# The order of the first two batches: what runs when, and where idle products stand

## The chip, the core and the metric

The kernel runs on one core of a Trainium2 chip. The metric is the device time of one execution in microseconds (us). A core has five engines that run their own instruction queues in order and wait for each other by semaphores: PE (TensorE, matrix products), DVE (VectorE), ACT (ScalarE), POOL (GpSimd) and SP (SyncE, which here issues every load and store).

## The reference

Eight batches. In each, two attentions follow each other: 32 packed queries p attend to the 576 positions of k and v, and then the 576 queries q attend to the 32 packed results. Then a layer with three maxima, and an output layer.

```python
batch, n_heads, seq, head_dim = (8, 8, 576, 64)
n_pack = 32
...
def sm_attn(qq, kk, vv):
    s = scale * np.matmul(qq, kk.transpose(0, 1, 3, 2))
    s = s - np.max(s, axis=-1, keepdims=True)
    a = np.exp(s)
    a = a / (np.sum(a, axis=-1, keepdims=True) + 1e-09)
    return np.matmul(a, vv)
p_packed = sm_attn(p, k, v)
out = sm_attn(q, p_packed, p_packed)
...
h = np.maximum(np.maximum(x @ w1, x @ w2), x @ w3)
return (h @ w_out).astype(np.float32)
```

Here x is `out` with heads and batches laid out as 4608 rows of 512, w1 to w3 are 512 x 768, and w_out is 768 x 512.

## The kernel before

The whole program is a list of generators, and two strings of words say in which order they are advanced: START (lines 48 to 73) for batches 0 and 1 and the first steps of batch 2, LOOP (line 76) once for each batch from 2 on, with steps of the next batches among its own. `run` (line 619) takes a word, finds or begins its generator, and lets it issue instructions up to its next `yield`. There is no other scheduler: each engine's queue holds its instructions in the order of the words. A trailing v, g or a puts a step on DVE, POOL or ACT in place of its default.

The words, with batch b, row half r, column block j:

- k, v, q, w: loads by SP. `w02` is the third part of weight block 0, `w6x` is w_out. `q010` is one half of the positions of q.
- Sb, `scores` (line 243): products of p and k, 32 of them, into two PSUM buffers.
- Abr, `weigh_and_turn` (line 605), four steps: maximum over 576 and its negated factor (L266, L267, DVE), exponential with its sum (L271, ACT), transposes of the result (L296, L297, PE), copies (a1t, `copy`).
- Zbr: the inverse of the sum. Vbr, `values` (line 324): products with v, 40 for each r (L337), and pp. Kb, `packed`: one transpose (L352) and the copy to pt.
- Qb, `queries` (line 356): products with q. In batch 0 it has two steps, one for each half of the positions.
- Bbrh, `attend` (line 374): the second softmax, step by step: transposes from PSUM (L389), maxima (L393), subtraction (L395), exponential (L397), sums (L400), inverse, product (L409), transpose (L412), split into high and low part (a2h, a2l).
- Cjc, `convert` (line 177): each weight part is turned into its form by two ACT steps, a shift on DVE (L202) and an add on POOL (L206).
- Pbj, `project` (line 424): products of pt and a weight block (L439), and their split into ph (ACT) and pl (DVE).
- Nbj, `layer_in` (line 459): groups of six products (L475, 36 for each b and j). E: the running maxima. H: operands of the output layer. W: its weights. O, F: the output layer and its end.

Buffers matter here. Scores, second scores, and batch 1's transposes take turns on two large PSUM buffers (`ps_big`), so a step that writes one waits until the last reader of its former contents is done. k, v, q and a few intermediate tiles share eight buffers, staged weights six. SP keeps eight loads under way, and the ninth waits for the first.

A word In (`idle`, line 136) lets the next PE step that calls `rouse` (line 138) first issue n idle products of 128 columns, of the identity matrix with itself. They write the buffer that the step will fill next, in groups of at most 512 columns.

```python
def rouse(ps):
    k = ps.shape[-1] // P
    for i in range(0, idle[0], k):
        n = min(idle[0] - i, k)
        nc.tensor.matmul(
            out=ps[:, 0:n * P], lhsT=ident, rhs=ident.unsqueeze(1).to_broadcast([P, n, P]),
            start=True, stop=True,
        )
    idle[0] = 0
```

Of the kernel before, what the change touches and what calls it, by code (L numbers as in the profile page):

```python
# [45 lines left out]


START = """
k00 k01 w02 I10 S0 A00 A00 k10 w00 C00 k11 Z00 w22 A00 w01 A01 A01 v01 Z01 C00 C02 C00 C01 v00 I4 S1 A10 A10
q000 C00 A11 I7 A01 A01v V01 C02 C02 A00v Z10 C01 C01 V01 q010 V00 C02 V00 K0 A11 Z11 C01 C22 C22 C22 K0 I1 Q0  # L50
B000 C22 B000 B000 B000 B010 B010 B000 q011 q001 I8 Q0 B011 B010 B010 w12 B001 B000v B000 B000g C12 I3 P00 P00
k20 B001 k21 B011 v11 B001 w10 B011 B010 B010 B000 B000g P00 P00 B001 B011 C12 C12 S2 B001 B000 B001 v10 B001
w11 B010 A21 B001g q10 q11 A21 I10 N00 A20 A20 B011 B010g B010 C12 B011 B011 B011g A10 A11 A10 A11 w21 C11 C11
V101 B010v C10 C10 B011 P00 B001 B001v w20 V101 B010 N00 E000 K1 w32 C11 K1v C10 N00 Q1 B001v C11 B10 C21 B11
C21 E000 E000 C20 N00 C10 P01 P01 B011g C21 C20 w42 C20 C32 w52 P01 B011 P10 X2 N00 N00 E001 E001 C32 C32 C42
C42 C42 C52 C21 w31 N01 E010v C20 w30 C31 C31 E001 B11 N01 v20 E010 N01 P02 C32 E010 C42 C31 C31 N01 w41 N01
w40 P02 P02 C30 E011 E011 C52 C52 N01 C30 P10 C30 X2 C41 C41 N02 P10 E011 N02 E020 E020 C30 B10 N02 C40 C41
Z21 E020 P03 P03 N02 E021 N02 w50 C50 C52 P03 N02 N03 N03 B10 w51 E021 E021 H01 N03 C50 C50 C40 C40 H00v B10
C41 B10 B10 B10 B11v N03 E031v C51 C51 C40 P04 E030v C51 C51 P11 P04 w64 B11 X2 E030 N03 N03 P04 N04 E031 E040
B11 B11 H02v N04 H02 C50 P05 v21 B10g E040 B11 B10 E031 C64 P05 B11g N04 N04 B11 B11 w61 N04 E041v C64 B10g  # L60
P05 B10 N04 C64 B11 w65 C61 w63 V201 E041 C65 C65 E040 E041 H04 H04 N10 E100v C65 N10 C61 C61 E100 Z20 V201
E030 N10 N10 N10 N10 C65 E101v P11 P11 N11 C64 q20 E101 q21 E101 w60 C60 C61 C60 E100 H04v E110v C60 C60 N11
N11 E110 E110 H10 N11 E111 W2v K2 w62 N11 E111 H10g K2 W0v W0 Q2 B20 B21 N11 N05 C63 H01v H00 C62 C62 C62 P13
E050 C63 W0v E111 B20 P12 P12 N05 C62 N05 N05 W0 E050 W2v E050 P12 W0v W2 N05 N05 N12 E051 H00 C63 C63 P13 W1
E120 N12 N12 E051 E051 N12 N12 W0 P14 B21 W2 P13 E120 E120 H03 P15 W2v W2g N12 E121 E121 W0v H01 W1 W1 W1 H02
N13 E121 N13 E130v E130 N13 N13 P14 N13 W1v W1 O0 P14 F0 E130 B20 O0 E131v N13 E131 H03v N14 N14 W1v H03v E131
W1v P15 B21 N14 E140v E140 W1g W1 W2v B21 B21 E140 F0 N14 O0 E141v P15 F0 O0 N14 N14 H05 H05v B20 H05v E141
H03 F0 H01 N15 O0 H12 N15 B20 H05 H13 E150v H01 W0 W2 O0 E141 F0 k30 F0 H03 H01v H14 H05 N15 N15 E151 E150
H03v N15 H05v E150 N15 O0 O0 H12 W0g E151 E151 H15 H13 H12v F0 O0 W2 H14 H13v W0v k31 F0 F0 O0 O0 O0 F0 F0 W2
O0 F0 F0 F0 H10v H14v H11 O0 O1 F1 O1 O1 F1 F1 B20v H15v F0 H15 B21 H11v H11v H13v H13 F0 H13v P20 H11 H11 P20  # L70
P20 H15 P22 P21 B21 P20 P20 O1 F1 H11v H15v O1 O1 H15v F1 F1 O1 B20 B20g O1 O1 F1 O1 F1 F1 B21g B21 B21 O1 F1
F1 O1 P22 P22 B21 P21 O1 F1 B20 P21 F1 B20 O1 F1 F1 B20v F1
"""


# [612 lines left out]
```

## Time and profile before

| | |
|---|---|
| median of 3 runs | 472.93 us (472.85 to 473.01) |
| the profiled execution: its time | 472.98 us |
| its span in the profile | 471.2 us |
| PE busy, share of the span | 457.2 us, 97% |
| DVE, ACT, POOL busy | 343.6, 168.4, 218.6 us |
| mean granted TensorE clock | 0.991 |
| DMA, GB/s in the first 47 us, in slices of 11.8 us | 332, 373, 379, 285 |

The profiled execution is a single one, and its span is measured from the first to the last recorded instruction. PE's share is close to full, but idle products count as busy, and so do products at a lower clock. Times within the execution are counted from the start of the span. "mi" are the products of the layer, "mo" those of the output layer, "s" scores of either kind, "tp" transposes, "av" products with v, "pw" projections. The figure in brackets at a row's end is the engine's idle time ahead of it and what ended it. In a row, x32 counts instructions, and an f32 product is two of them. The granted clock is given as a share of full speed.

### The profile page before, as it was taken

To read this page: it belongs to the slowest core of one execution; us is meant where nothing else is said; L and a number is where in the kernel's file an instruction comes from. 1 tells how busy PE (TensorE), PEld (TensorE's weight loads), DVE (VectorE), ACT (ScalarE), POOL (GpSimd) and SP (SyncE) were. 2 spreads that over 40 slices of the span, in tenths; PEclk is the share of its full clock that TensorE was granted. 3 is DMA by queue.
4 is the path that set the end of the run, shared out by engine and by line. 5 is a ranking of instruction groups with operands and counts; after the bars stand their busy time and mean duration, and the time that the engine had idled before them with its cause. 6 is when DMAs were issued, how large, how long until landed. Compare 5 with 4: busy or idle time off the path is not lost.

```text
span 471.2 us, 11512 instructions
## 1 busy us (share of the span) xinstructions
PE 457.2 (97%) x4710; PEld 404.1 (86%) x4710; DVE 343.6 (73%) x722; ACT 168.4 (36%) x325; POOL 218.6 (46%) x193
## 2 busy tenths in 40 slices
PE   7799999999999999999999999999999999999996
PEld 2447887899989898989989898998989898998996
DVE  1669986987888678786777678776787667875652
ACT  3458855634233226122350225212260223402330
POOL 0467784776544055612564037421556036531642
PEclk9889999999999999999999999999999999999999
DMA  8998856002213640082303730064300820020002
GB/s 332 373 379 285 293 159 245 1 1 86 86 65 119 199 127 1 25 282 51 111 1 101 229 105 35 26 204 118 120 1 34 280 41 3 26 75 1 1 4 98
DMA packets 36580, 55.66 MB, mean 118 GB/s; under 512 B 17328, under 2 KB 27568, under 8 KB 36528
## 3 DMA queue, kind: packets, MB, share of 16 engines
q1 hardware_dynamic: 36528, 54.93, 35.4%
q8 instruction: 37, 0.61, 0.5%
q14 instruction: 15, 0.12, 0.1%
HBM read 41.94 MB, written 9.44 MB: 109 GB/s over the span
## 4 chain that ended last, share of the span: by engine, by line
PE 87%; DMA 6%; DVE 3%; ACT 1%; issue 1%; POOL 1%; SPq 1%; DVEq 0%; ACTq 0%; POOLq 0%
PE mi L475 45%; PE mo L544 29%; PE pw L439 7%; DMA wi<-in_wi 3%; DMA v<-in_va 2%; PE av L337 2%; DMA wi<-in_wo 2%; PE s L366 2%; PE s L253 1%; PE s L143 1%; DVE e L389 1%; DVE w_sb L202 1%; DVE r L489 0%; DVE xt L218 0%; PE tp L296 0%
## 5 line engine op out<-in xcount | busy, mean ns | idle before, releaser
L475 PE MATMUL mi<-a2h,ph 128*128 128x288 f32 x576 | 174.0, 302 | 0.6 <-ACT r L129 0.5
L475 PE MATMUL mi<-a2h,pl 128*128 128x288 f32 x576 | 170.0, 295 | 0.2 <-DVE pl L452 0.2
L475 PE MATMUL mi<-a2l,ph 128*128 128x288 f32 x576 | 169.8, 295 | 0.0
L475 PEld LDWEIGHTS mi<-a2h,ph 128*128 128x128 f32 x576 | 108.1, 188 | 15.6 <-issue 9.9
L475 PEld LDWEIGHTS mi<-a2h,pl 128*128 128x128 f32 x576 | 108.1, 188 | 0.7 <-DVE pl L452 0.7
L489 DVE TENSOR_TENSOR r<-mi,r 128x288 f32<-128x288 f32 x192 | 84.2, 449 | 33.3 <-PE mi L475 29.8
L475 PEld LDWEIGHTS mi<-a2l,ph 128*128 128x128 f32 x576 | 108.1, 188 | 0.0
L129 ACT COPY r<-mi 128x288 f32<-128x288 f32 x54 | 20.9, 398 | 120.3 <-PE mi L475 117.2
L452 DVE SCALAR_TENSOR_TENSOR pl<-pw,ph 128x768 fp32r<-128x768 f32 (+1 forms) x61 | 46.6, 772 | 3.2 <-ACT ph L450 2.6
L450 ACT ACTIVATE ph<-pw 128x768 fp32r<-128x768 f32 (+1 forms) x61 | 39.8, 674 | 15.2 <-PE pw L439 14.7
L513 POOL TENSOR_TENSOR r<-r 128x576 f32<-128x576 f32 (+1 forms) x29 | 35.2, 1225 | 20.5 <-issue 9.0
L544 PE MATMUL mo<-ych,xh 128*128 128x288 f32 x144 | 42.5, 295 | 0.0
L544 PE MATMUL mo<-ycl,xh 128*128 128x288 f32 x144 | 42.5, 295 | 0.0
L544 PE MATMUL mo<-ych,xl 128*128 128x288 f32 x144 | 42.4, 295 | 0.0
L134 POOL TENSOR_TENSOR yal<-r,yah 128x576 fp32r<-128x576 f32 x14 | 20.2, 1443 | 47.1 <-ACT yah L129 39.3
L439 PE MATMUL pw<-w_sb,pt 64*32 64x384 f32 x768 | 36.1, 487 | 0.8 <-POOL w_sb L206 0.4
L271 ACT ACTIVATE a<-s,nm 128x576 f32<-128x576 f32 x16 | 11.8, 740 | 65.9 <-DVE nm L267 65.9
L206 POOL TENSOR_TENSOR w_sb<-w_sb,wi 128x512 int32<-128x512 int32 x18 | 23.7, 1326 | 23.2 <-DVE w_sb L202 16.3
L131 DVE COPY r<-mi 128x288 f32<-128x288 f32 x42 | 18.9, 453 | 18.4 <-PE mi L475 18.3
L131 POOL CAST yah<-r 128x576 fp32r<-128x576 f32 x7 | 4.7, 674 | 56.4 <-DVE r L513 56.4
L544 PE MATMUL mo<-yah,xh 128*128 128x288 f32 x96 | 28.9, 301 | 0.0
L544 PE MATMUL mo<-ybl,xh 128*128 128x288 f32 x96 | 28.3, 295 | 0.0
(121 smaller groups left out, 871.6 us busy)
## 6 DMA issues: line engine op xcount, KB each, us to landing
kt<-in_kp SPq DMA_DIRECT2D x16, 640.0 KB, 4.0
wi<-in_wi SPq DMA_DIRECT2D x18, 512.0 KB, 7.6
v<-in_va SPq DMA_DIRECT2D x16, 512.0 KB, 5.7
q<-in_qt SPq DMA_DIRECT2D x14, 576.0 KB, 7.0
wi<-in_wo SPq DMA_DIRECT2D x6, 512.0 KB, 6.1
out_t<-r SPq DMA_DIRECT2D x8, 288.0 KB, 2.4
out_t<-t SPq DMA_DIRECT2D x8, 288.0 KB, 2.3
out_t<-s SPq DMA_DIRECT2D x8, 288.0 KB, 2.7
```

Of the source, the lines that this page charges most:

```text
L129: e.copy(out=out, in_=src)
L131: e.tensor_copy(out=out, in_=src)
L134: on(default).tensor_tensor(out=lo, in0=src, in1=hi.bitcast(F32), op=ALU.subtract)
L206: nc.gpsimd.tensor_tensor(out=dst.bitcast(I32), in0=dst.bitcast(I32), in1=up, op=ALU.add)
L271: nc.scalar.activation(out=a.rearrange("p (a b) -> p a b", a=2), in_=s[:, :, 0:HS], func=AF.Exp, bias=nm, scale=SCALE, accum_out=z,)
L439: nc.tensor.matmul(out=ps[r][NP * n:NP * n + NP, 0:NW * P], lhsT=pt_sb[b % 2][o, NP * n:NP * n + NP], rhs=w_sb[o, j, n * NW * P:(n + 1) * ...
L450: nc.scalar.activation(out=hi[:, r], in_=x, func=AF.Copy, scale=2.0 ** -WS)
L452: nc.vector.scalar_tensor_tensor(out=lo[:, r], in0=x, scalar=2.0 ** -WS, in1=hi[:, r].bitcast(F32), op0=ALU.mult, op1=ALU.subtract,)
L475: nc.tensor.matmul(out=sums[b, j, hf, x][:, 0:HS], lhsT=w[:, r, x * P:(x + 1) * P], rhs=a[:, c], start=(r == 0 and n == 0), stop=(r == R - ...
L489: nc.vector.tensor_tensor(out=h, in0=sums[b, j, hf, i][:, 0:HS], in1=h, op=ALU.max)
L513: less = lambda out, x, y: on("g").tensor_tensor(out=out, in0=x, in1=y, op=ALU.subtract)
L544: nc.tensor.matmul(out=ps[:, 0:HS], lhsT=w[:, x, m * P:(m + 1) * P], rhs=h[:, z], start=(p == 0 and i == 0), stop=(p == NQ - 1 and i == 2),)
```

## The change

Only the string START differs. It holds the same words in another order, except for the idle words and some letters that choose an engine: I had 10, 4, 7, 1, 8, 3, 10 products (43), and has 10, 10, 1, 9, 2, 5, 3, 1 (41).

```diff
 START = """
-k00 k01 w02 I10 S0 A00 A00 k10 w00 C00 k11 Z00 w22 A00 w01 A01 A01 v01 Z01 C00 C02 C00 C01 v00 I4 S1 A10 A10
-q000 C00 A11 I7 A01 A01v V01 C02 C02 A00v Z10 C01 C01 V01 q010 V00 C02 V00 K0 A11 Z11 C01 C22 C22 C22 K0 I1 Q0
+k00 k01 I10 S0 A01 A01 I10 A01 A00 A00 v01 w00 C00 q010 v00 q000 A01 I1 A00 A00v C00 C00 I9 V00 Z00 q001 V00
+V01 Z01 V01 K0 w01 K0v C01 I2 Q0 B010 B010 q011 Q0 C01 k11 k10 C01 B001 B001 B000 B011 B000 B011 w02 B000v
...
 """
```

SP's queue at its start, before (kt0 and kt1 are k of batch 0, kt2 and kt3 of batch 1, wi2_2 is part 2 of weight block 2, v0 and v1 are v of batch 0):

```order
L159 DMA kt0_79<-in_kp 128x1280
L159 DMA kt1_81<-in_kp 128x1280
L153 DMA wi0_2_83<-in_wi 128x512
L159 DMA kt2_113<-in_kp 128x1280
L153 DMA wi0_0_115<-in_wi 128x512
L159 DMA kt3_118<-in_kp 128x1280
L153 DMA wi2_2_123<-in_wi 128x512
L153 DMA wi0_1_132<-in_wi 128x512
L165 DMA v1_141<-in_va 128x1024
L166 DMA v1_141<-in_vb 64x256
L165 DMA v0_151<-in_va 128x1024
L166 DMA v0_151<-in_vb 64x256
```

and with the change:

```order
L159 DMA kt0_79<-in_kp 128x1280
L159 DMA kt1_81<-in_kp 128x1280
L165 DMA v1_128<-in_va 128x1024
L166 DMA v1_128<-in_vb 64x256
L153 DMA wi0_0_131<-in_wi 128x512
L174 DMA q1_134<-in_qt 128x2x288
L165 DMA v0_136<-in_va 128x1024
L166 DMA v0_136<-in_vb 64x256
L174 DMA q0_139<-in_qt 128x2x288 x2
L153 DMA wi0_1_211<-in_wi 128x512
L174 DMA q1_134<-in_qt 128x2x288
L159 DMA kt3_240<-in_kp 128x1280
```

v and q of batch 0 moved ahead of k of batch 1 and of three weight parts.

PE's queue around the scores of batch 1 (s1_1), before:

```order
L296 MATMUL tp0_0_125<-ident_67,a1_0_0_110 128x128 x4
L297 MATMUL pa0_0_126<-ident_67,a1_0_0_110 64x128
L143 MATMUL s1_1_0_154<-ident_67 128x512
L253 MATMUL s1_1_0_154<-kt2_113 32x288
L253 MATMUL s1_1_1_155<-kt2_113 32x288
```

and with the change, where s2_0_1 is the second half of the second scores of batch 0:

```order
L366 MATMUL s2_0_1_230<-q0_139,pt0_73 32x288 x4
L366 MATMUL s2_0_1_230<-q1_134,pt0_73 32x288 x4
L143 MATMUL s1_1_0_271<-ident_67 128x512
L143 MATMUL s1_1_0_271<-ident_67 128x128
L253 MATMUL s1_1_0_271<-kt2_242 32x288
L253 MATMUL s1_1_1_272<-kt2_242 32x288
```

The scores of batch 1 moved from behind the first transposes of batch 0 to behind its second scores. The scores of batch 2 then follow at once, with P00 behind them; before, P00 stood ahead of them.

DVE's queue around the maxima of those scores (mx1_0, mx1_1), before:

```order
L202 TENSOR_SCALAR w_sb_72<-wi0_0_115 128x512
L266 TENSOR_REDUCE mx1_0_173<-s1_1_0_154 128x1
L267 TENSOR_SCALAR nm1_0_174<-mx1_0_173 128x1
L266 TENSOR_REDUCE mx1_1_183<-s1_1_1_155 128x1
L267 TENSOR_SCALAR nm1_1_184<-mx1_1_183 128x1
L131 COPY a1t0_1_196<-tp0_1_187 128x512
```

and with the change:

```order
L389 STREAM_TRANSPOSE e0_0_245<-s2_0_0_215 128x288
L389 STREAM_TRANSPOSE e0_1_225<-s2_0_1_230 128x288
L393 TENSOR_REDUCE m2_0_0_0_251<-e0_0_245 128x9
L393 TENSOR_REDUCE m2_0_1_288_253<-e0_1_225 128x9
L395 TENSOR_TENSOR e0_0_245<-e0_0_245,m2_0_0_0_251 128x288
L395 TENSOR_TENSOR e0_1_225<-e0_1_225,m2_0_1_288_253 128x288
L400 TENSOR_REDUCE z2_0_1_0_265<-e0_1_225 128x9
L400 TENSOR_REDUCE z2_0_0_0_268<-e0_0_245 128x9
L405 TENSOR_SCALAR z2_0_0_0_268<-z2_0_0_0_268 128x9
L266 TENSOR_REDUCE mx1_0_318<-s1_1_0_271 128x1
L267 TENSOR_SCALAR nm1_0_319<-mx1_0_318 128x1
L202 TENSOR_SCALAR w_sb_72<-wi0_2_255 128x512
```

The maxima of batch 1 moved from ahead of batch 0's first copies into its second softmax.

More of the change, by code (lines that the diff above doesn't have):

```diff
@@ L48 @@
 START = """
-k00 k01 w02 I10 S0 A00 A00 k10 w00 C00 k11 Z00 w22 A00 w01 A01 A01 v01 Z01 C00 C02 C00 C01 v00 I4 S1 A10 A10
-q000 C00 A11 I7 A01 A01v V01 C02 C02 A00v Z10 C01 C01 V01 q010 V00 C02 V00 K0 A11 Z11 C01 C22 C22 C22 K0 I1 Q0
-B000 C22 B000 B000 B000 B010 B010 B000 q011 q001 I8 Q0 B011 B010 B010 w12 B001 B000v B000 B000g C12 I3 P00 P00
-k20 B001 k21 B011 v11 B001 w10 B011 B010 B010 B000 B000g P00 P00 B001 B011 C12 C12 S2 B001 B000 B001 v10 B001
-w11 B010 A21 B001g q10 q11 A21 I10 N00 A20 A20 B011 B010g B010 C12 B011 B011 B011g A10 A11 A10 A11 w21 C11 C11
@@ L54 @@
[L54 to L72, printed above, removed]
+k00 k01 I10 S0 A01 A01 I10 A01 A00 A00 v01 w00 C00 q010 v00 q000 A01 I1 A00 A00v C00 C00 I9 V00 Z00 q001 V00
@@ new lines @@
+V01 Z01 V01 K0 w01 K0v C01 I2 Q0 B010 B010 q011 Q0 C01 k11 k10 C01 B001 B001 B000 B011 B000 B011 w02 B000v
+B011v C00 k21 B010 C01 B010 B010 B000 B000 B000v I5 S1 B011 k20 w12 C02 C02 I3 S2 B001 A10 B001 C02 C02 P00
+B010v A11 A10 A11 B011 B010 B011 C12 B000 P00 B010g Z10 C12 B011 B010 w11 B010v B000g B000 v10 B001 A21 B001v
+P00 P00 A11 Z11 B001 A20 B001g B011g B000v w10 v11 B000v A21 A10 B001 q10 C12 B001v A20 C10 N00 w21 B011 B010v
+A10 A11 I1 V101 C10 B011 P00 N00 V101 C11 C11 B001v C11 C12 E000 q11 N00 C21 K1 C21 w20 N00 C10 K1v Q1 E000
@@ new lines @@
+E000 C20 C20 C21 w22 Z20 B011 N00 w30 B10 C22 C11 C10 P01 P01 N00 E001 w31 B11 B11 C21 C20 C20 C22 C22 C22 w50
+C30 P01 w32 B10 C31 C30 P10 w41 X2 B10v N01 E010 C30 N01 C31 P02 P02 C31 w40 C32 N01 E001 E010 E001 C30 N01
+N01 E011 C32 B11 C31 P02 C32 C32 E010 N02 v21 E011 N02 v20 N02 N02 w42 w52 B10 X2 H00 E020 E020 E020 B11 B11
+B11v C40 C40 C40 C40 C41 C41 P03 N02 C41 P03 E021v P03 N01 N02 E021 w51 C42 C42 N03 N03 B10 X2 C41 B11 C52 B10
+P10 w64 E011 C50 N03 C42 C42 E030v P10 H00 B10 Z21 N03 C52 P04 B11g P11 P04 E031 E021 E030 P04 N03 B10g w62
@@ new lines @@
+C52 N03 E030 N04 N04 E031 B11 C51 C51 B10 E040 E031 C52 E040 w65 H00 C50 B11 B11v P11 C51 N04 N04 B10 B10v N04
+N04 E041 C64 C64 E041 E041 E040 C51 N10 C62 H02v E100 N10 N10 C50 C50 V201 q20 P11 P05 H03v w63 H02 C65 C65
+C65 N11 E110 C64 C64 H03v C65 N11 N10 E100 V201 K2 E110 P05 C62 W2 N10 P05 E100 E101v C62 w60 H02v C63 N11
+E110 H03v K2 q21 Q2 B21 N05 N05 C63 C63 B20 H01 E050 C63 N10 B20 B20 C60 P13 E050 W2 E101 C60 E101 P12 P13 W2
+N05 H04v N05 P13 E050 C62 N11 E111 C60 N11 E111 B20 N11 W1v H03v P12 W1 P12 N13 E111 E051 N05 E051 H04 N05 N12
@@ new lines @@
+E051 C60 E130 N13 W1 N13 N12 W2 W2v P15 w61 C61 C61 C61 E120v E120 E130 P14 W1 W1v N13 C61 W0v W0v N12 E120
+N12 W2 N13 H05g N12 W2 W2 P15 E130 H03 N12 E131 P15 B21 E121 E121 E131 P14 P14 N15 N15 N15 W0 N13 E150 E150
+N14 N14 W2 N14 N14 N15 N15 E121 H03v H05 W2 W0 W0v E131 N14 W1 E150 E140 E140 E140 W0 W0 W0 H13 H04v H05 B20
+E151v B20 O0 N14 E141v E141 E151 W1v N15 H01v E141 W0 k30 O0 F0 H10 O0 F0 O0 O0 O0 E151 H05v H10 W1 k31 P20
+B20 H01 F0 H01v F0 W0v H10v P21 H05 B21v F0 H01 H05v P22 H01v F0 H12 H11 H14v O0 W1g H11v O0 H11v P21 B21 F0
@@ L73 @@
+O0 O0 H13 P20 P20 P20 H11v F0 H12 H12v B20 O0 F0 F0 F0 F0 H13 W1v P20 O0 B20 O0 O0 H14 F0 H14v F0 F0 B21 O1 F0
+H15 H15v H15 O1 H11 B21 H13v F1 F1 H15v H15 H13v P22 O1 F1 H11v O1 H13v H15v O1 B20 F1 O1 O1 B20 O1 F1 B21
+B21g P21 O1 O1 F1 F1 F1 F1 F1 F1 F1 P22 B21 O1 F1 O1 O1 F1 B21 B21 F1 O1 F1
 """
```

## The prediction

> **What bounds the kernel now.** The table of stretches comes first. Its columns are the length, the busy time of PE (with its instructions), PEld, DVE, ACT and POOL, the granted TensorE clock, and the DMA share with GB/s.
>
> ```profile
> 7.50:31.40 23.90, 18.76 (x224) 8.72 (x224) 14.62 (x43) 11.96 (x27) 9.63 (x11) 0.86 1.04 379
> 41.30:90.00 48.70, 46.93 (x519) 39.31 (x519) 42.58 (x93) 33.20 (x59) 34.82 (x30) 1.00 0.59 198
> 90.00:420.00 330.00, 330.00 (x3405) 302.50 (x3404) 251.91 (x513) 103.03 (x200) 149.34 (x126) 1.00 0.29 89
> ```
>
> From 90 us on PE is never idle, and the real products are the same before and after. So the change is worth exactly what it does to the time in which PE does no real product ahead of 90 us: idle time, idle products, and products at a low clock. The next view is PE's timeline of that part (start, length, what, idle time ahead of it).
>
> ```profile
> 5.81 1.67 PE L253 MATMUL s<-kt 64*32 64x288 f32 x32
> 9.46 0.66 PE L296 MATMUL tp<-ident,a 128*128 128x128 f32 x4 [1.98 <-ACT a L271]
> 13.14 1.77 PE L143 MATMUL tp<-ident 128*128 128x512 f32 x4
> 18.01 0.90 PE L337 MATMUL av<-v,a1t 128*32 128x64 f32 x40 [2.55 <-DMA v<-in_va]
> 20.37 0.48 PE L352 MATMUL av<-ident,pp 128*128 128x128 f32 x1 [0.44 <-DVE z L282]
> 21.20 1.21 PE L366 MATMUL s<-q,pt 64*32 64x288 f32 x16
> 22.34 3.78 PE L143 MATMUL s<-ident 128*128 128x512 f32 x4
> 26.05 0.72 PE L366 MATMUL s<-q,pt 64*32 64x288 f32 x16
> 27.54 0.88 PE L439 MATMUL pw<-w_sb,pt 64*32 64x384 f32 x16
> 28.21 1.18 PE L253 MATMUL s<-kt 64*32 64x288 f32 x32
> 31.38 0.48 PE L475 MATMUL mi<-a2h,ph 128*128 128x288 f32 x1
> 34.95 1.81 PE L337 MATMUL tp<-v,a1t 128*32 128x64 f32 x80
> 38.69 1.20 PE L366 MATMUL s<-q,pt 64*32 64x288 f32 x32
> 41.29 1.52 PE L439 MATMUL pw<-w_sb,pt 64*32 64x384 f32 x32 [0.41 <-POOL w_sb L206]
> ```
>
> Here the products with v (V01, V00) wait for a late load until 18.01, eight idle products stand in front of the second half of Q0, and the first layer product comes at 31.38. I use 41.29, the start of P01, as the **mark**: what is done by then can be counted in both orders. Afterwards three waits remain (by the list of waits: total, times, longest):
>
> ```profile
> PE s L366 <- ACT pt L129: 1.0, 1, 1.0
> PE pw L439 <- DVE e L389: 0.4, 1, 0.4
> PE mi L475 <- DVE pl L452: 0.2, 1, 0.2
> ```
>
> That is 1.6 us, and it is all that can be won behind the mark.
>
> **The loads.** The queue's issues, with sizes and median time to landing:
>
> ```profile
> kt<-in_kp SPq DMA_DIRECT2D x16, 640.0 KB, 4.0
> wi<-in_wi SPq DMA_DIRECT2D x18, 512.0 KB, 7.6
> v<-in_va SPq DMA_DIRECT2D x16, 512.0 KB, 5.7
> q<-in_qt SPq DMA_DIRECT2D x4, 288.0 KB, 7.6
> ```
>
> Up to and with the second v there were four k, four w and two v: 5.6 MB, landed at about 17.9. Now there are two k, one w, one half q and two v: 3.1 MB, so 55% of it, 10 to 12 us, 13.6 if it lags further. The nine idle products before V00 end later than that (below). At the same rate I estimate k of batch 1 at 18 to 20, w02 at 20 to 21.5 and k of batch 2 at 23 to 25, each before its user in the sum below, the closest by about 1 us. On POOL, the add that finishes w02 follows a shift that stands right behind the first maximum of S1, so it lies beside S2. So loads no longer bound, and I cost them at nothing; if that cover fails, the price is 1 to 2 us.
>
> **The new front, at full clock.** Seven products took 1.77, so ten take 2.2 without the tail of the last. S0 ends at 7.5 as before, since its two loads still come first. The transposes of r1 follow the ten products (9.65; the exponential is done at 9.4, as for r0 in the row at 9.46), those of r0 wait for theirs (10.3). The vector engine's copies (0.69 and 0.27, their rows are below) end at 12.1. Nine products go to 14.2, V00 and V01 (1.81 for 80 in the row at 34.95) to 16.0. K0 (0.48) with the two short vector steps around it goes to 17.1, an estimate, and two halves of Q0 at 0.72 to **18.5**. Before, the second half ended at 26.8. So 8.3 us are gained there, but they don't reach the mark, for this work now stands in a row on the vector engine:
>
> ```profile
> 14.13 0.75 DVE L266 TENSOR_REDUCE mx<-s 128x1 f32<-128x576 f32 x1
> 14.91 0.15 DVE L267 TENSOR_SCALAR nm<-mx 128x1 f32<-128x1 f32 x1
> 16.19 0.41 DVE L202 TENSOR_SCALAR w_sb<-wi 128x512 uint32<-128x512 uint32 x1
> 15.39 0.69 DVE L131 COPY a1t<-tp 128x512 f32<-128x512 f32 x1 [0.33 <-PE tp L296]
> 16.00 0.27 DVE L131 COPY a1t<-pa 64x128 f32<-64x128 f32 x1
> 22.52 0.48 DVE L389 STREAM_TRANSPOSE e<-s 128x288 f32<-128x288 f32 x1 [1.61 <-PE s L366]
> 23.04 0.45 DVE L393 TENSOR_REDUCE m<-e 128x9 f32<-128x288 f32 x1
> 43.11 0.96 DVE L452 SCALAR_TENSOR_TENSOR pl<-pw,ph 128x768 fp32r<-128x768 f32 x1
> ```
>
> ```profile
> 11.01 0.72 ACT L271 ACTIVATE a<-s,nm 128x576 f32<-128x576 f32 x1
> 11.63 0.19 ACT L271 ACTIVATION_READ_ACCUMULATOR a<-s,nm 128x1 f32 x1
> 42.26 0.81 ACT L450 ACTIVATE ph<-pw 128x768 fp32r<-128x768 f32 x1 [2.27 <-PE pw L439]
> ```
>
> S1 used to run at 10 to 13, in the shadow of the late v, with its maxima on an idle vector engine. It now writes the buffers of Q0, so it waits until batch 0's transposes have read them. From 17.95 that is six instructions (three transposes, two maxima, one shift), to 20.6. PE idles 2.1 us there and can't run the five products earlier, since they write the same buffer. They end at 21.8, S1 (1.18) at 23.0. Eight more vector instructions, then the maximum and its factor (0.75 and 0.15) to 24.4, the exponential with its sum (0.72, 0.19) to 25.3: only now is S2's first buffer free, and the second at 26.85. S2 ends at 28.0, P00 (0.88) at 28.9. The transposes of batch 1 take S2's buffers and wait for two more maxima and exponentials: the first is free near 31.3, the second later. From 17.95 to the last vector result that the first layer product needs stand 41 instructions; 14.62 us for 43 in the first row above is 0.34 each, so 13.9: 31.9. With the exponential PE gets on at 32.5, and the first product comes at **33.1**, 1.7 later than before. Then its other five products, V101 34.3 to 36.0, and to P01 four groups of six layer products, K1 and Q1:
>
> ```profile
> 109.70 2.40 PE mi L475 x18
> ```
>
> Six cost 0.80. So 36.0 + 4×0.80 + 0.2 + 1.2 = 40.6, and P01 starts at **40.7**, with one group more done than before: 41.29 − 40.7 + 0.8 = **1.4 gained** at the mark. Behind it the new order puts one group and P10 (1.6 us) between P01 and the first use of its low part, which needs 0.81 + 0.96 and the hand-overs: a wait of 0.7, and some 0.5 at P02 in the same way. I keep 0.3 of the old 1.6 (the loads of w_out now come a little earlier). At full clock the sum is −1.4 + 1.2 + 0.3 − 1.6 = **−1.5**.
>
> **The clock.** The same table in stretches of 3.41 us, laid so that the falls and rises lie on their edges:
>
> ```profile
> 5.65:9.06 3.41, 1.83 (x33) 0.59 (x32) 0.91 (x2) 0.48 (x1) 0.00 (x0) 1.00 1.02 419
> 15.88:19.29 3.41, 1.28 (x72) 1.13 (x72) 2.68 (x9) 3.07 (x8) 2.13 (x2) 1.00 1.03 305
> 19.29:22.70 3.41, 2.97 (x44) 1.43 (x33) 1.03 (x5) 0.27 (x1) 1.73 (x2) 0.50 1.07 404
> 22.70:26.11 3.41, 3.41 (x12) 0.87 (x16) 2.05 (x5) 1.40 (x3) 1.34 (x2) 0.50 1.01 408
> ```
>
> A stretch with 54% busy PE changed nothing. One with 38%, a 2.55 us gap in it, was followed by half clock, 87% busy didn't lift it, and 100% did. At half clock a half of Q0 took 1.21 for 0.72, and eight products 3.78. The new order has gaps of 2.1 (18.5 to 20.6), 2.3 (23.0 to 25.3) and 2.4 us (28.9 to 31.3). In the stretch 22.70 to 26.11 PE would be busy 1.05 us, 31%. So I take it that the clock is halved from 26.1. Then S2 costs 1.1 more and P00 0.8, of which 1.65 reach the first product through pl and the maxima; two transposes add 0.45, the first six products 0.7, V101 with its copies 0.5, the next products 0.2: **3.5**, if the full stretch 36.3 to 39.75 lifts the clock. PE is then so late that the 1.2 of new waits vanish: −1.4 + 3.5 + 0.3 − 1.6 = **+0.8**.
>
> The Trainium skill, "TensorE: Matmul & The Clock Gate", section "HAM oscillation — how this bites in real kernels", says that idle gaps up to about 3.4 us leave the clock up. By that rule the time would be that of rival 1; the 2.55 us gap of this trace, with 0.50 behind it, speaks against it.
>
> **The rivals.**
> - 1, **the clock stays up**: −1.5, 471.5 us. For it: the edges may lie elsewhere, and a gap of 2.0 at 7.5 did no harm. Against it: three gaps, of which nearly every position of the edges catches one.
> - 2, **slower: the half clock lasts** to 43.2, because V101's small products don't count as full work, as the 87% row suggests. Its price at the mark is 5.2 for 3.5: +2.5, 475.5 us. It decides for slower as soon as the clock isn't back by 39.75. A load that comes too late for S2 or P00 would end in the same place.
> - 3, **the vector engine isn't the bound**: if its 41 instructions overlap better than 0.34, up to 3.6 us of the 8.3 survive: 468 to 470.5 us.
>
> **How the numbers follow.** The profiled execution took 472.98 us, its span 471.2, so 1.8 lie around it and stay; it stands 0.05 above the median of 472.93. The forecast is the clock's fall with a return at 39.75: 472.93 + 0.8 = **473.7**. It has chance 0.39, with 472.5 to 474.9 for its own range, since the return may come at 36.3 (0.9 less) or the vector chain be off by 1. Rival 1 has 0.29, rival 2 0.22, rival 3 0.10. About 0.2%, 0.95 us, is what a measurement of this kernel can tell from no change. Faster by more: 0.03 of the forecast, 0.21 of rival 1, all of rival 3: 0.34. Slower by more: 0.14 of the forecast, 0.01 and 0.20 of the rivals: 0.35. Within: 0.31. The range 469.8 to 476.2 takes in both bounds of the clock's return and part of rival 3, and leaves out the rest of rival 3 and what lies beyond rival 2.
>
> **What would show it.** Right: the second half of Q0 ends near 18.5; PE idles near 19.5, 24 and 30; the granted clock is 0.5 from about 26; the first layer product comes behind 33; no wait of a microsecond in 70 to 90 us. Wrong: a clock of 1.0 throughout (rival 1), 0.5 beyond 40 (rival 2), a first layer product before 31 (rival 3), or a wait of PE for a load of k or w ahead of 30 us, which would break the step on the loads.

## The result, and the profile after

| | before | with the change |
|---|---|---|
| median (20 runs each, beside each other) | 472.85 us (470.13 to 474.56) | 475.25 us (471.90 to 477.61) |
| ratio, 95% interval | | 1.0059 (1.0039 to 1.0080) |
| a second time, beside the experiments | 472.86 us | 474.79 us, 1.0044 (1.0018 to 1.0070) |
| profiled execution: time, span | 472.98, 471.2 us | 472.88, 471.1 us |
| its mean granted clock | 0.991 | 0.996 |
| its PE busy | 457.2 us | 453.5 us |

The change makes the kernel slower by 0.6%, 2.4 us at the median. The first profiled execution of it doesn't show that: it took 472.88 us, among the fastest of its runs. What sets it apart is in the mean granted clock, which every run reports. Here are all 34 runs of the change, those of the experiments included, by that clock:

| mean clock | runs | time, us: lowest, median, highest |
|---|---|---|
| 0.994 to 0.996 | 5 | 471.90, 472.88, 473.05 |
| 0.991 to 0.993 | 6 | 473.43, 474.44, 474.98 |
| 0.985 to 0.989 | 17 | 474.22, 476.24, 477.61 |
| 0.978 to 0.982 | 6 | 476.81, 477.14, 477.53 |

One stretch of 3.41 us at half clock takes 0.5 x 3.41 / 471 = 0.0036 off the mean. So 0.996 is one such stretch, 0.989 three, 0.978 six. Two slow runs, one of the kernel before (1077.48 us) and one of experiment 8 (737.95 us), are left out of all medians and ratios. Three profiles of the change are shown here, of executions with 0.996, 0.989 and 0.978, and called the first, second and third; a fourth was like the first.

The table of stretches for the first one, with the same columns as before the change:

```profile
7.50:31.40 23.90, 15.93 (x233) 8.74 (x230) 16.81 (x55) 12.10 (x28) 7.54 (x9) 0.98 1.03 377
41.30:90.00 48.70, 45.50 (x511) 37.69 (x512) 41.67 (x88) 32.45 (x60) 30.64 (x26) 1.00 0.63 204
```

PE is busy for less time in the front (15.93 us for 18.76, fewer products at half clock) and waits longer behind it: 48.70 - 45.50 = 3.20 us without products in the second stretch, for 1.77 before. PE's timeline of the same execution shows where:

```profile
17.29 1.21 PE L366 MATMUL s<-q,pt 64*32 64x288 f32 x32
20.83 1.32 PE L143 MATMUL s<-ident 128*128 128x512 f32 x4 [2.33 <-DVE e L389]
25.29 0.91 PE L143 MATMUL s<-ident 128*128 128x384 f32 x2 [2.02 <-ACT a L271]
30.68 1.11 PE L296 MATMUL tp<-ident,a 128*128 128x128 f32 x4 [2.27 <-ACT a L271]
32.93 0.59 PE L475 MATMUL mi<-a2h,ph 128*128 128x288 f32 x1
41.81 0.88 PE L439 MATMUL pw<-w_sb,pt 64*32 64x384 f32 x16 [0.98 <-POOL w_sb L206]
75.63 0.40 PE L475 MATMUL mi<-a2h,ph 128*128 128x288 f32 x1 [1.91 <-DVE r L489]
79.80 1.17 PE L366 MATMUL s<-q,pt 64*32 64x288 f32 x24 [0.78 <-DMA q<-in_qt]
```

Q0 ends at 18.5, the three gaps follow, the first layer product stands at 32.93 and P01, the mark, at 41.81. The wait of P01 for GpSimd's add of its weights grew from 0.41 to 0.98 us, a layer product at 75.63 now waits for a maximum, and Q2 waits 0.78 for a load where it waited 1.0 for its copy to pt.

Where the half clock lies is read from the table in stretches of 3.41 us, laid on its edges. The first profile:

```profile
16.86:20.27 3.41, 1.63 (x35) 0.58 (x33) 2.38 (x7) 0.30 (x1) 1.11 (x2) 1.00 1.02 408
20.27:23.68 3.41, 2.45 (x36) 1.17 (x36) 3.38 (x11) 1.66 (x5) 1.54 (x2) 1.00 1.02 414
23.68:27.09 3.41, 1.80 (x21) 0.78 (x29) 2.95 (x13) 2.96 (x8) 2.15 (x3) 1.00 1.03 394
27.09:30.50 3.41, 1.33 (x38) 0.46 (x22) 3.31 (x12) 2.13 (x6) 0.56 (x2) 1.00 1.05 346
30.50:33.91 3.41, 3.23 (x14) 2.80 (x15) 3.34 (x9) 2.12 (x7) 2.26 (x3) 0.50 1.01 381
33.91:37.32 3.41, 3.41 (x96) 3.11 (x95) 2.36 (x7) 3.15 (x8) 1.11 (x2) 1.00 1.02 409
```

The edges happen to cut the first two gaps in two, so the stretches stay 48%, 72% and 53% busy. Only the third gap lies in one stretch (39%), and one stretch of half clock follows.

### The profile page after: what moved, and what is told of

The parts are those of the page before. It is cut to its first block, busy times and chain, and to the rows that moved or that the text cites. A ratio compares the mean times of both kernels' runs of the same rounds, so it can differ in the third digit from the quotient of the medians.

```text
span 471.1 us, 11501 instructions
## 1 busy us (share of the span) xinstructions
PE 453.5 (96%) x4714; PEld 404.0 (86%) x4714; DVE 346.9 (74%) x727; ACT 171.7 (36%) x333; POOL 207.0 (44%) x180
## 4 chain that ended last, share of the span: by engine, by line
PE 93%; DVE 3%; DMA 2%; ACT 1%; issue 0%; POOL 0%; POOLq 0%; DVEq 0%
PE mi L475 48%; PE mo L544 29%; PE pw L439 7%; PE s L253 2%; DMA q<-in_qt 2%; PE av L337 2%; PE s L366 2%; PE s L143 1%; PE tp L296 1%; DVE e L389 1%; PE tp L143 1%; DVE xt L218 0%; PE pa L143 0%; PE pa L337 0%; DVE w_sb L202 0%
## 5 line engine op out<-in xcount | busy, mean ns | idle before, releaser
L489 DVE TENSOR_TENSOR r<-mi,r 128x288 f32<-128x288 f32 x192 | 83.2, 449 | 33.8 <-PE mi L475 31.0
L129 ACT COPY r<-mi 128x288 f32<-128x288 f32 x60 | 23.3, 399 | 121.4 <-PE mi L475 121.3
L134 POOL TENSOR_TENSOR yal<-r,yah 128x576 fp32r<-128x576 f32 x13 | 18.6, 1430 | 47.0 <-ACT yah L129 47.0
L513 POOL TENSOR_TENSOR r<-r 128x288 f32<-128x288 f32 (+1 forms) x25 | 27.8, 1126 | 17.5 <-issue 9.0
L131 DVE COPY r<-mi 128x288 f32<-128x288 f32 x36 | 16.3, 454 | 16.5 <-PE mi L475 16.5
L544 PE MATMUL mo<-ybh,xl 128*128 128x288 f32 x96 | 28.3, 295 | 0.0
```

The source lines that it names most:

```text
L129: e.copy(out=out, in_=src)
L131: e.tensor_copy(out=out, in_=src)
L134: on(default).tensor_tensor(out=lo, in0=src, in1=hi.bitcast(F32), op=ALU.subtract)
L489: nc.vector.tensor_tensor(out=h, in0=sums[b, j, hf, i][:, 0:HS], in1=h, op=ALU.max)
L513: less = lambda out, x, y: on("g").tensor_tensor(out=out, in0=x, in1=y, op=ALU.subtract)
L544: nc.tensor.matmul(out=ps[:, 0:HS], lhsT=w[:, x, m * P:(m + 1) * P], rhs=h[:, z], start=(p == 0 and i == 0), stop=(p == NQ - 1 and i == 2),)
```

## The experiments

All kernels ran beside the kernel before, which gave medians of 472.99, 472.86 and 473.24 us. Where a time is compared with the change, 475.25 and 474.79 are meant. "Rn" is a word added for the experiments: n idle products at once, into one of the four small PSUM buffers, so that they need not wait for a large one. (In experiments 4, 11 and 12 those ahead of V01 wait 0.7 us for a small one.)

```python
if kind == "R":
    idle[0] = int(name[1:])
    rouse(ps_moe.tile([P, 512], F32, name=f"idle{len(begun)}", tag="moe"))
    continue
```

**1. The change with its three gaps filled.**

```diff
-... I5 S1 ... I3 S2 ... P00 B010v A11 A10 A11 ...
+... R10 I5 S1 ... R9 I3 S2 ... P00 B010v R10 A11 A10 A11 ...
```

> The change, with idle products also in the three gaps of PE ahead of the first layer product: 10 behind Q0, 9 behind S1, 10 behind P00, into an unused small buffer, so that they need not wait for the large ones. The idle products of the change stay. Nothing on the other engines differs. Theory (the half clock, of a length that differs from run to run, is what the change loses): mean clock at least 0.998 in nearly all runs, no spread over 1 us, and the profiled run's 472.88 less 1.6 for its one halved stretch: 471.3 us, that is 0.992 of the change. Rival (the vector engine's row and the later waits cost it, and the clock is the same in the change as before): the gaps stay as long, the time stays at 475 and the spread at 5 us.

Measured: 472.13 us (470.93 to 473.05), ratio to before 0.9984 (0.9964 to 1.0004). Seven of the twelve runs have a mean clock of 0.999 or 1.0 (median 471.23), five 0.994 to 0.996 (472.87). PE's timeline:

```profile
18.19 2.42 PE L143 MATMUL idle<-ident 128*128 128x512 f32 x6
20.59 1.32 PE L143 MATMUL s<-ident 128*128 128x512 f32 x4
22.97 2.21 PE L143 MATMUL idle<-ident 128*128 128x512 f32 x6
25.06 0.91 PE L143 MATMUL s<-ident 128*128 128x384 f32 x2
28.11 2.42 PE L143 MATMUL idle<-ident 128*128 128x512 f32 x6
32.24 0.38 PE L475 MATMUL mi<-a2h,ph 128*128 128x288 f32 x1
40.99 0.88 PE L439 MATMUL pw<-w_sb,pt 64*32 64x384 f32 x16 [0.98 <-POOL w_sb L206]
```

The gaps are as long as before, only filled: S1 begins at 20.59 (20.83 in the first profile) and S2 at 25.06 (25.29). Real work is neither removed nor moved, and 2.7 to 3.1 us go. So half clock is the loss at the median, and the gaps cause it. The level is 0.8 above the expected 471.3, and the clock is at least 0.998 in seven runs where nearly all were expected. A spread of 2.1 us is left, for the expected 1; where the five runs with 0.994 to 0.996 lose their clock wasn't seen.

**2. The change without the idle products behind the first two gaps.**

```diff
-... I5 S1 ... I3 S2 ...
+... S1 ... S2 ...
```

> The change without the five idle products ahead of S1 and the three ahead of S2, which stand behind the waits and so on the path. Theory of the clock: 1.8 us of products less on the path at full clock, but the stretches of the two gaps are emptier, the clock falls in more runs and earlier (mean clock 0.985 to 0.990): 474 to 476 us, no clear gain on 475.25. Rival (the idle products there are a plain cost, and the clock goes its own way): 473.4 us, 1.8 less than the change, at the same mean clocks.

Measured: 474.79 us (474.23 to 476.60), ratio 1.0044 (1.0024 to 1.0063), mean clock 0.978 to 0.989 with a median of 0.986. As the theory of the clock has it: eight products less on the path, and no gain. The half clock of its profile lies at 23.02 to 29.85, at 33.26 to 36.67 and, behind the waits near 75 us, at 77.63 to 81.05.

**3. The gaps filled, and those eight left out.**

```diff
-... I5 S1 ... I3 S2 ... P00 B010v A11 A10 A11 ...
+... R10 S1 ... R9 S2 ... P00 B010v R10 A11 A10 A11 ...
```

> The change with the 29 idle products in the three gaps, and without the eight behind the first two waits. Theory of the clock: clock 1.0 as in the run with both, and S1 and S2 earlier by 1.1 and 0.7: 469.5 to 470.0 us, about 1.5 below the run with both. Rival (vector row): the earlier S1 and S2 only lengthen the next gap, time as in the run with both.

Measured: 471.76 us (471.05 to 473.75), ratio 0.9978 (0.9956 to 1.0001), 0.4 below experiment 1 where 1.5 were expected. The rival is right: PE's timeline shows S2 wait twice for the exponentials of S1, at 25.39 and 26.67, 0.6 us each. At full clock the eight products stand in the shadow of that chain.

**4. The kernel before, with its wait for v filled.**

```diff
-... A01v V01 C02 C02 ...
+... A01v R12 V01 C02 C02 ...
```

> The kernel before, with 12 idle products in its wait for v ahead of V01 (2.55 us), into an unused small buffer. Theory: the stretch that held this gap was 38% busy and was followed by 6.8 us of half clock; filled, the clock stays at 1.0 and the 6.4 us that PE was busy there shrink by some 2 to 3 us: 470 to 471 us, mean clock 0.998, and a narrower spread than before's 4.4. Rival (the loads set the time of this part, and the half clock lies in their shadow): 472.5 to 473, with the mean clock up all the same.

Measured: 471.98 us (470.66 to 472.86), ratio 0.9960 to 0.9996 around 0.9978; mean clock 0.994 to 1.0, where the kernel before beside it had 0.987 to 0.995. The clock rises as expected, the time falls by 1.0 us instead of 2 to 3. In its timeline the twelve products run to 20.00, 2 us past the 18.01 at which V01 began before: too many by about eight. One stretch of half clock is left in it, from 10.66 to 14.07, behind a stretch that the gap of 1.99 us after S0 left 42% busy. In the profile before, with the stretches elsewhere, the same gap changed nothing. Experiments 11 and 12 fill it too.

**5. The change once more**, unchanged.

> The change itself, once more, beside the kernels below. Theory (each stretch of 3.41 us whose products stand still for 2 us or more can be followed by half clock, and where the stretches begin differs from run to run): time goes with the mean clock, 0.996 (one halved stretch) 472 to 473, 0.989 (three) 474.5 to 475.5, 0.978 (six) about 477, median 475.2; in the profiled run every halved stretch lies between 20 and 45 us and behind one that was less than 60% busy. Rival: runs of the same mean clock differ by more than 2 us, or halved stretches lie elsewhere.

Measured: 474.79 us (472.86 to 477.53). Its profile was again one of 0.996, with the same rows. Time follows the clock, but the spread at 0.989 is 474.2 to 477.1 here and to 477.6 in all: in this the rival is right, a count of stretches doesn't settle the time.

**6. The filled change, with the steps of w_out later.** At 75 us PE waits for a maximum, queued on the vector engine behind two shifts of w_out parts that ScalarE converts late; ScalarE itself waits for the load of one. ScalarE's row and then the vector engine's, from the first profile of the change:

```profile
70.39 0.71 ACT L188 ACTIVATE wi<-wi 128x512 f32<-128x512 f32 x1 [3.70 <-DMA wi<-in_wo]
73.78 0.76 DVE L202 TENSOR_SCALAR xb<-wi 128x512 uint32<-128x512 uint32 x2 [2.82 <-ACT wi L188]
```

```diff
-... H02 C65 C65 C65 N11 E110 C64 C64 H03v C65 N11 N10 E100 V201 K2 E110 P05 ...
+... H02 C65 C65 N11 E110 H03v N11 N10 E100 V201 K2 E110 C65 C64 C64 C65 P05 ...
```

> The change with the idle products in its three gaps, and with the vector and GpSimd steps of the first two w_out parts (C64, C65) moved behind the maxima (E110, E100) and the products with v of batch 2 (V201). In the trace the vector engine stood 2.4 us for a w_out part that ScalarE had late, and PE waited 1.5 us for the maximum queued behind it, at 74 us. Theory: that wait goes and nothing else is late: 1.5 us below the run with the idle products alone, 470.6 us. Rival: the next wait (the projections' low part, or the load of q at 78 us) takes its place: 471.5 to 472.

Measured: 471.75 us (471.05 to 474.89), ratio 0.9986 (0.9966 to 1.0006). PE's list of waits:

```profile
PE s L366 <- DMA q<-in_qt: 1.1, 1, 1.1
PE pw L439 <- POOL w_sb L206: 1.0, 1, 1.0
PE s L366 <- ACT pt L129: 0.8, 1, 0.8
...
PE mi L475 <- DVE r L489: 0.3, 1, 0.3
```

The rival is right. The waits for maxima fell from 1.7 to 0.3 in all, and Q2, the next step, now waits for the copy to pt and for the load of q: 1.9 us in place of 0.4.

**7. The kernel before, with v loaded earlier**: one part of the change alone.

```diff
-... k11 Z00 w22 A00 w01 A01 A01 v01 Z01 C00 C02 C00 C01 v00 I4 S1 ...
+... k11 v01 v00 Z00 w22 A00 w01 A01 A01 Z01 C00 C02 C00 C01 I4 S1 ...
```

> The kernel before with one thing of the change: both v of batch 0 are loaded ahead of two weight parts (1 MB, 2.6 us at 390 GB/s). No product moves. Theory: the 2.55 us wait for v ahead of V01 falls to under 0.5, so the clock does not fall at 19.3, and the first layer product comes 2 to 3 us sooner, unless the weights are late: 470 to 471.5 us, mean clock above 0.997. Rival: the two parts that are late now hold up P00 and P01, time 473 or more with the clock up all the same.

Measured: 475.11 us (473.75 to 477.75), ratio 1.0053 (1.0033 to 1.0072), mean clock 0.985 to 0.993. ScalarE's rows of its timeline first, then PE's:

```profile
18.99 0.67 ACT L188 ACTIVATE wi<-wi 128x512 f32<-128x512 f32 x1 [5.42 <-DMA wi<-in_wi]
19.56 0.72 ACT L271 ACTIVATE a<-s,nm 128x576 f32<-128x576 f32 x1
20.18 0.19 ACT L271 ACTIVATION_READ_ACCUMULATOR a<-s,nm 128x1 f32 x1
20.42 1.45 PE L337 MATMUL av<-v,a1t 128*32 128x64 f32 x40 [3.87 <-ACT a L271]
```

Neither holds in full. V01 no longer waits for v, but its buffer is that of S1, which the exponential of batch 1 must read first, and that stands on ScalarE behind the conversion of a weight part that is now late. The wait grew from 2.55 to 3.87, and half clock followed it again, from 20.47 to 27.30 (another stretch of it, from 10.23, lies behind the gap after S0). So late parts cost time, though not at P00 or P01 as the rival had it. Here a load moved alone left other steps queued behind one that is now late.

**8. The change, with S1 and its softmax back ahead of Q0.**

```diff
-... q010 v00 q000 A01 ... K0v C01 I2 Q0 ... C01 k11 k10 C01 ... I5 S1 ... S2 B001 A10 B001 ... B010v A11 A10 A11 ...
+... q010 v00 q000 k11 k10 A01 ... K0v C01 S1 A11 A10 A11 A10 I2 Q0 ... C01 C01 ... S2 B001 B001 ... B010v ...
```

> The change with the scores of batch 1 and their maxima and exponentials (S1, A10, A11) put back ahead of the second scores of batch 0 (Q0), and k of batch 1 loaded right behind v and q of batch 0. Idle words stay, without the five of S1. Theory (what kept the 8.3 us that Q0 gained from the first layer product is S1 behind it, with its maxima in the vector engine's row and its buffers): Q0 ends near 22.5, the gaps behind Q0 and S1 become one, and the first layer product comes at 31 to 32 instead of 33.3; with one gap fewer the clock is up more often: 472 to 473.5 us. Rival (loads and conversions bind the mark whatever the order): PE waits at P00 or P01 for weight parts that are 3 us later, 474 to 476.

Measured: 478.27 us (five runs, 477.07 to 478.79), ratio 1.0106 (1.0081 to 1.0132), mean clock 0.978 to 0.986. PE's timeline:

```profile
19.82 1.22 PE L143 MATMUL s<-ident 128*128 128x256 f32 x2 [2.06 <-ACT a L271]
25.01 0.89 PE L143 MATMUL s<-ident 128*128 128x384 f32 x2 [1.95 <-DVE e L389]
29.70 1.50 PE L439 MATMUL pw<-w_sb,pt 64*32 64x384 f32 x8 [0.83 <-POOL w_sb L206]
33.62 1.11 PE L296 MATMUL tp<-ident,a 128*128 128x128 f32 x4 [2.42 <-ACT a L271]
36.31 0.59 PE L475 MATMUL mi<-a2h,ph 128*128 128x288 f32 x1
```

The theory falls: the gaps don't merge. Whoever takes the two large buffers next waits two microseconds for their last readers, in both orders of S1 and Q0, and a weight part is late besides.

**9 and 10. Two more profiles of the change**, of executions that are not among the fastest.

> The change itself, one look, to see where the half clock lies in a run that is not among its fastest. Theory: halved stretches of 3.41 us only between 16 and 45 us, each behind a stretch in which the gaps at 18.5, 23.1 and 28.4 us leave the products busy for less than 60%, and ended by one that is over 90% busy; the time is 471.3 us plus what the products in them were stretched by, 1 to 1.7 us for each. Rival: they begin behind stretches that are over 70% busy, or come behind 50 us.

> The change itself, a second look, with the same expectation as the first.

Measured: 477.40 us at a mean clock of 0.989, and 477.08 at 0.978. The second profile in stretches:

```profile
17.65:21.06 3.41, 1.14 (x32) 0.43 (x32) 2.58 (x7) 0.44 (x1) 1.60 (x2) 1.00 1.02 408
21.06:24.48 3.42, 3.35 (x20) 1.63 (x28) 2.64 (x8) 2.01 (x5) 1.06 (x2) 0.50 1.02 411
24.48:27.89 3.41, 1.37 (x26) 0.43 (x10) 2.54 (x8) 1.37 (x4) 1.18 (x1) 1.00 1.04 377
27.89:31.30 3.41, 3.41 (x49) 1.62 (x48) 2.60 (x10) 1.21 (x4) 1.40 (x3) 0.50 1.05 380
31.30:34.71 3.41, 1.12 (x13) 0.50 (x5) 2.77 (x11) 2.78 (x7) 1.33 (x2) 1.00 1.01 392
34.71:38.13 3.42, 3.21 (x18) 2.92 (x21) 3.29 (x7) 2.58 (x8) 1.36 (x2) 0.50 0.60 241
```

Here each gap lies whole in a stretch (33%, 40%, 33% busy), and each is followed by half clock, just where the products stand. Full clock falls on the gaps. The third:

```profile
18.65:22.07 3.42, 1.38 (x12) 0.81 (x20) 3.39 (x10) 0.48 (x2) 2.66 (x3) 1.00 1.02 412
22.07:25.48 3.41, 2.00 (x32) 0.59 (x27) 2.52 (x9) 2.55 (x6) 0.00 (x0) 0.50 1.02 407
25.48:28.90 3.42, 2.86 (x26) 1.17 (x34) 2.97 (x13) 2.00 (x6) 2.58 (x3) 0.50 1.04 369
28.90:32.31 3.41, 2.18 (x32) 0.44 (x16) 1.93 (x6) 1.14 (x3) 0.00 (x0) 0.50 1.03 361
32.31:35.72 3.41, 2.35 (x11) 2.23 (x12) 3.31 (x11) 2.41 (x6) 1.81 (x3) 0.50 1.02 407
35.72:39.14 3.42, 3.42 (x69) 3.20 (x71) 1.67 (x3) 3.34 (x8) 1.69 (x2) 0.50 0.79 279
```

One fall behind a stretch of 40%, and then four stretches of 59 to 84% don't lift it, until a full one does at 39.14. PE's timeline of this third profile at the mark:

```profile
45.54 0.88 PE L439 MATMUL pw<-w_sb,pt 64*32 64x384 f32 x16 [0.97 <-POOL w_sb L206]
```

The second has P01 at 45.35, with the same wait of 0.99. Five stretches of half clock lie in this table, six in the mean clock. The sixth comes behind the mark, after a wait of 1.90 us for the maximum at 79.78:

```profile
76.68:80.10 3.42, 1.38 (x8) 1.15 (x9) 2.17 (x7) 3.34 (x7) 1.19 (x1) 1.00 1.02 410
80.10:83.51 3.41, 3.41 (x16) 3.39 (x15) 3.41 (x7) 1.96 (x4) 2.41 (x3) 0.50 0.62 224
```

In this the rival is right: half clock comes behind 50 us too, and the waits there have a price in the clock as well. The price was above the expected 1 to 1.7 for each stretch in the second profile (477.40 - 471.3 = 6.1 for three), and 1.0 in the third (5.8 for six).

**11 and 12. The kernel before, with two early gaps filled**: 9 products behind S0, 5 ahead of V01. The first also drops the eight in front of the second half of Q0.

```diff
-... I10 S0 A00 A00 ... A01v V01 ... q011 q001 I8 Q0 ...
+... I10 S0 R9 A00 A00 ... A01v R5 V01 ... q011 q001 Q0 ...
```

> The kernel before with idle products in its two early gaps (9 behind S0, 5 ahead of V01), and without the eight in front of the second half of Q0, which no wait covers. Theory (at full clock those eight cost their 1.8 us on the way to the first layer product): mean clock at least 0.998, V01 near 18, the second half of Q0 ends near 22.5 and the first layer product comes near 29: 469.5 to 470.5 us. Rival (the mark is bound by the weights of block 1): the wait of P01 for GpSimd's add grows by what is won ahead of it, and the time is that of the run with the eight, within 0.5.

> As the run before it, but with the eight idle products left in front of the second half of Q0. Theory: mean clock at least 0.998 and 471 us, a little under the run with twelve idle products in front of V01, whose excess pushed V01 from 18 to 20. Rival: 472 as there, since what comes earlier waits at P01.

Measured: 471.02 us (469.87 to 472.50), ratio 0.9962 (0.9945 to 0.9979), and with the eight 470.99 us (469.23 to 472.37), ratio 0.9960 (0.9939 to 0.9981). Of the 24 runs 23 have a mean clock of 0.998 or more. Both are faster than the kernel before by 0.4% and than the change by 0.9% (471.0 for 475.25). The eight products cost nothing, as the rival had it, but at another place. PE's timeline of the first:

```profile
25.49 0.81 PE L253 MATMUL s<-kt 64*32 64x288 f32 x8 [0.51 <-DMA kt<-in_kp]
27.27 1.18 PE L253 MATMUL s<-kt 64*32 64x288 f32 x24 [0.97 <-DMA kt<-in_kp]
30.44 0.48 PE L475 MATMUL mi<-a2h,ph 128*128 128x288 f32 x1
```

Q0 ends 2.3 us earlier without the eight, and S2 then waits for k of batch 2. The wait of P01 is 0.4, as before.

These runs allow a comparison of the two orders at the same clock. The seven runs of experiment 1 with 0.999 or more have a median of 471.23 us, beside 472.99 for the kernel before; the old order with its gaps filled has 471.0, beside 473.24. So at full clock the new order gains nothing that these runs can tell.

## Why the prediction was right, and where it fell short

The sign of the forecast and its range hold, the size doesn't: +0.8 was forecast, +2.4 measured. The sign was in good part luck, since the prediction itself gave faster and slower nearly the same chance (0.34 and 0.35). That the median lies next to the 475.5 of rival 2 doesn't confirm that rival. It had half clock last from 26.1 to 43.2, because V101's small products don't lift the clock, and no profile of the change shows this: in the third, V101 begins at 37.56, in the very stretch that lifted it. Point by point:

- **Loads no longer bind: right in the front.** PE waits for no load ahead of 30 us but once, 0.2 for k of batch 0 in the third profile. Experiment 7 shows that the load of v moved alone, without the steps that go with it, makes the kernel slower. Behind the mark loads do bind, where they were costed at nothing: a part of w_out, for which ScalarE stood 3.70 us, and q, for which PE stood 0.78 (first profile).
- **The new front: right.** Q0 ends at 18.5 in the first profile, as said, and the gaps are 2.33, 2.02 and 2.27 us for 2.1, 2.3 and 2.4. They hardly change with the clock (2.34, 1.97 and 2.29 in the third profile), so what the products between them lose comes on top.
- **At full clock the mark at 40.7: right within 0.3.** Experiment 1, at clock 1.0, has P01 at 40.99, and 0.98 us of it is a wait for GpSimd's add (0.41 before) that the sum didn't have. The first layer product comes at 32.24, earlier than the 33.1, so this wait eats what was won.
- **Three gaps halve the clock: right, and shown** by experiment 1. Its level, 472.13, is close to rival 1's 471.5, the time for a clock that stays up. The forecast had half clock from 26.1 to 39.75: the third profile has it from 22.07 to 39.14. In the first it is one stretch, in the second three apart.
- **Its price at the mark, 3.5, was too small.** Against experiment 1's 40.99, P01 comes 0.8, 4.4 and 4.6 later in the three profiles. By the table of clocks, 23 of 34 runs have 0.989 or less. The forecast put one position of the stretches in the sum and began the half clock behind the first gap's products; where S1 falls under it too (1.63 and 2.13 us for 1.20), the price is larger by one.
- **The step that failed: "PE is then so late that the 1.2 of new waits vanish", with the old 1.6 won.** They don't, and the sign "no wait of a microsecond in 70 to 90 us" failed with them: there is one of 1.9 us in each of the three profiles. In the stretch from 41.30 to 90, apart from the wait of P01, PE is without products for 2.7, 3.2 and 2.1 us in the three profiles, 1.9 in experiment 1, and 1.8 before. So nothing was won behind the mark, where -1.3 stood in the sum. The waits weren't those named (low parts at pl), but a maximum behind w_out's conversion, and q. In the third profile half clock follows there too (80.10 to 83.51). Experiment 6 removed the larger, and Q2's copy and load took its place: this part of the program is held by several things at once.

The third profile makes the account. At the mark, 45.54 - 41.29 - 0.8 for the group done ahead = 3.45 us are lost (forecast: 2.1). From the mark to the end of its span the kernel before took 471.2 - 41.29 = 429.9, so with one group less 429.1 would be even. It took 475.3 - 45.54 = 429.8, so 0.7 is lost behind the mark (forecast: -1.3). Together that is the 4.1 by which the span is longer. By the same account the second profile loses 3.3 and 1.1, the first wins 0.3 and loses 0.1, and experiment 1, with its gaps filled, wins 1.1 and 0.7.

- **Rival 3** (the vector engine isn't the bound) found no support: the gaps stood. That the maxima's place was the cause, which the forecast's working suggests, wasn't borne out either: experiment 8 moved them forward and the gaps stayed.
- **The Trainium skill's limit of 3.4 us for an idle gap** ("TensorE: Matmul & The Clock Gate", "HAM oscillation — how this bites in real kernels") doesn't hold here: gaps of 2.0 to 2.3 us were enough in the second profile. The Trainium skill says on the same page, in "What's actually happening", that the activity window is free-running. The edges at 30.50, 21.06 and 22.07 in three executions of one program agree with that.

Open are the spread at equal mean clock (474.2 to 477.6 at 0.985 to 0.989), and what binds the waits between 70 and 80 us beyond those seen in experiment 6. Where the stretches fall may be part of that spread: in the second profile half clock lies just on the products and full clock on the gaps. It was not measured.

## What to carry to other kernels

A gap of PE is priced by what it does to the clock behind it as well as by its length, and the price is a distribution, since the stretches begin elsewhere in each execution: look at the clock of all runs, not at one profile. Idle products belong into a gap, in a buffer that is free, and sized to end with it; behind the first two waits of the change eight of them did nothing (474.79 us without them). A product order that wins 8 us in front (Q0 at 18.5 for 26.8) wins only what the next shared buffer, weight part or load lets through.

## What the runs showed of the hardware that was not expected

- The bounds of the clock's rule, over all profiles. From 3 us on, the clock fell behind every stretch of 3.41 us at full clock in which PE was busy for 43% or less (33, 38, 39, 40, 42 and 43% among them), and behind none with 52% or more. Between these it went both ways: it fell behind 47% (experiment 2, 19.61 to 23.02) and 50% (experiment 8, 77.46 to 80.87), and not behind 45% (experiment 5, 16.90 to 20.31) and 48% (first profile). So PE's busy share alone doesn't settle it there. The clock rose behind 89% (experiment 8, 19.43 to 22.85), 94, 95, 98 and 100%, and not behind 87% or less (59, 64, 69 and 84% in the third profile). So half clock, once there, survives work with moderate gaps, as in the third profile for five stretches.
- The profiled run of experiment 3 reported a clock of 0.949, from 10 us on 0.95 throughout. Its layer products took 302 and 295 ns as in the others, its projections 502 for 487, and its time, 473.24 us, is within the spread. What 0.95 stands for was not found.
